# One column's transpose placed inside the first up unit, its copy shared by two engines, and the first up weights loaded in halves

## Chip, cores and metric

The kernel runs on one core of a Trainium2 chip. The metric is the device time of one execution in microseconds (us); of several executions the median is taken.

## What is computed

The input `x` has 2048 rows (the sequence) of 512 values. Each row is normalised, and the result is the sum of the input, a spectral filter and a gated MLP:

```
xn  = layernorm(x)                                   # over the 512 values
A   = irfft2(rfft2(xn) * (w_r + 1j * w_i))           # over rows and values
g   = xn @ w_gate        # 2048x512 @ 512x1792
u   = xn @ w_up          # 2048x512 @ 512x1792
B   = (gelu(g) * u) @ w_down                         # back to 2048x512
out = x + A + B
```

All inputs are bf16. The change touches the layer norm and the `g` and `u` products only in the order of their first pieces.

## The kernel before

The 2048 rows lie in 16 columns of 128 rows (`NC = 16`; column `c` holds rows `16p + c`). Every column is normalised with its rows on the partitions (`xn`) and then transposed into `xnT`, with the 512 values on the partitions in four blocks of 128 (`NE = 4`, index `e`), because the matmuls contract over the values. Columns 0 to 3 are transposed on TensorE (`f_T`, L346, into a PSUM tile `tp`) and copied to SBUF by VectorE or ScalarE (`f_Tc`, L351). The other twelve are transposed by DMA (L450).

The gated MLP is cut into units (`unit`, L465). A unit takes `n` columns and `m` blocks of 128 of the 1792 hidden values: it computes a gate part (`g_ps`) and an up part (`u_ps`) on TensorE, the gelu on ScalarE (`ge`, L498) and the product on VectorE (`hT`, L503). `g_ps` and `u_ps` have two PSUM buffers each: the gelu gives a `g_ps` buffer back and the product a `u_ps` buffer. The list `todo` (L530) gives the order: unit 0 is column 0 with hidden blocks 0 to 3, unit 1 is column 1 with the same blocks, units 2 and 3 are columns 0 and 1 with blocks 4 and 5 and then 6 and 7, and then come columns 2 and 3 and the rest. Unit 0 runs `mm_half` (L488), which goes over the value blocks `e` in two halves; every other unit runs `split`, which calls `mm` (L480), with the hidden block outside and `e` inside.

The spectral filter (forward transforms, groups of frequencies, inverse transform) is put between the units later on, and the down product closes the kernel (L811).

The order of each engine's instructions is written by a small planner (`Plan`, L135). Every step has an engine, a duration, a latency, a key and its dependencies; `t_min` is the earliest time and holds an expected landing time of the data (`LAND`, `WG_LAND`, `WU_LAND`, L309). The planner simulates and picks the ready step with the lowest key; the chip then runs each engine's list strictly in that order. The planner gives no times to the chip, only the order.

The opening (L274) is outside the planner. SyncE (SP) issues nearly all loads in the order written. ScalarE issues the first gate weights. Waits that are added when the program is built make a DMA wait, before it is issued, for an earlier one: eight completion semaphores go round, so that in the kernel before the load of columns 2 and 3 waits for column 0, the gate weights 512 to 1023 for column 1, and the up weights 512 to 1023 for the first quarter of the first up weights. TensorE runs 37 matmuls on zeros (L307) while it waits for data.

The steps near the change, as the list of each engine has them before:

- TensorE: transposes of column 0, six matmuls on zeros (L322), gate 0, up 0 (16 matmuls each), four transposes of column 1, gate 1, up 1, gate 2, up 2, eight transposes of columns 2 and 3, gate 3 and so on without another transpose.
- VectorE: statistics and normalisation of columns 0 and 1 (L337 to L343), one copy of the transposed column 1, statistics of columns 2 and 3, the products of units 0 and 1, normalisation of columns 2 and 3, the product of unit 2.
- ScalarE: two square roots (L392) and the copies of column 0 (L352), then a load of the gelu table and the gelus of units 0, 1 and 2.
- GpSimd: the inverse root for columns 2 and 3 (L355, L359), between their statistics and their normalisation.

```
for e in range(NE):
    load_w(Wu_sb, 0, 512, e=e)
...
t = add("PE", 0.23, lambda: f_T(1, 0, NE), [o["xn1"]], key=-1998, lat=0.45, acq=("S",))
...
v("copyt", lambda: f_Tc(1, 0, NE), 0.5, ["t"])
```

Of the kernel before, what the change touches and what calls it, by code (L numbers as in the profile page):

```python
# [17 lines left out]
S = 2048  # L18
# [3 lines left out]
NE = 4  # L22
# [112 lines left out]
class Plan:  # L135
# [6 lines left out]
    def add(self, eng, occ, fn, deps=(), key=0.0, lat=None, slack=0.0, t_min=0.0, acq=(), rel=(), after=None):  # L142
        lat = occ + 0.25 if lat is None else lat
        op = Op(len(self.ops), eng, occ, lat, fn, [d for d in deps if d is not None], key, slack, t_min, acq, rel,
                after)
        self.ops.append(op)
        return op
# [54 lines left out]
def kernel(  # L202
# [11 lines left out]
    nc = tc.nc  # L214
# [17 lines left out]
    Wg_sb = pc.tile([P, NE, DF], BF16, name="Wg_sb")  # L232
    Wu_sb = pc.tile([P, NE, DF], BF16, name="Wu_sb")
# [14 lines left out]
    def load_consts(first, last):  # L248
        a, b = ccols[first][0], sum(ccols[last])
        nc.sync.dma_start(out=CT[:, a:b], in_=cap[:, a:b])  # L250


    def load_x(c0, n, eng=nc.sync):
        eng.dma_start(out=x_t[:, c0:c0 + n, :], in_=x_v[:, c0:c0 + n, :])

    def load_w(a, b, eng=nc.sync):
        nc.sync.dma_start(out=Wg_sb[:, :, a:b], in_=wg_v[:, :, a:b])
        eng.dma_start(out=Wu_sb[:, :, a:b], in_=wu_v[:, :, a:b])
# [15 lines left out]
    def opening():  # L274
        nc.vector.memset(spin[:], 0.0)
        nc.vector.memset(eps_t[:], EPS)
        nc.vector.memset(minus_half[:], -0.5)
        U = nc.gpsimd
        U.memset(ident_t[:], 1.0)
        U.affine_select(out=ident_t[:], in_=ident_t[:], pattern=[[-1, P]], compare_op=ALU.is_equal, fill=0.0,  # L280
                        base=0, channel_multiplier=1)
        nc.scalar.activation(out=warm[:], in_=eps_t[:], func=AF.Sqrt, bias=eps_t[:], scale=1.0)
        load_x(0, 1)
        load_x(1, 1)
        load_w(Wg_sb, 0, 512, nc.scalar, e=slice(0, 2))
        load_w(Wg_sb, 0, 512, nc.scalar, e=slice(2, 4))
        for e in range(NE):
            load_w(Wu_sb, 0, 512, e=e)
        load_x(2, 2)
        load_w(Wg_sb, 512, 1024)  # L290
        load_w(Wu_sb, 512, 1024)
        load_x(4, 4)
        load_w(Wg_sb, 1024, DF)
        load_w(Wu_sb, 1024, DF)
        load_x(8, 4)
        nc.sync.dma_start(out=RF_t[:], in_=rf_d.rearrange("p (c k) -> p c k", c=NC))
        load_x(12, 4)
        nc.sync.dma_start(out=idx_t[:], in_=nc.inline_tensor(idx_np, name="spec_rows").ap())
        load_consts("F0", "L0")
        load_consts("I0", "M0")  # L300
        for T, w_in in ((TR, A_w_r), (TI, A_w_i)):
            rows = w_in.rearrange("(kb a h g) k -> h kb a (g k)", kb=NC, h=2, a=8)
            Tf = T.rearrange("p j k -> p (j k)")
            for h in range(2):
                nc.sync.dma_start(out=Tf[64 * h:64 * h + 64, W:8 * W], in_=rows[h, :, 0:4, W:8 * W])
        for k in range(37):
            nc.tensor.matmul(sp_ps[:, :P], lhsT=spin[:], rhs=spin[:], start=True, stop=True)  # L307

    LAND = {0: 2.9, 1: 4.5, 2: 7.2, 3: 7.2}  # L309
    LAND.update({c: 11.5 if c < 8 else 17.5 if c < 12 else 20.5 for c in range(4, NC)})  # L310
    WG_LAND = [5.0] * 4 + [8.6] * 4 + [13.2] * 6
    WU_LAND = [6.7] * 4 + [10.0] * 4 + [15.2] * 6
    RF_LAND = 19.0

    ident = ident_t[:]
# [10 lines left out]
    add = plan.add  # L326
    V, A, T_ = nc.vector, nc.scalar, nc.tensor
# [18 lines left out]
    def f_T(c, e0, n):  # L346
        tiles["T", c, e0] = tp = ps.tile([P, n, P], BF16, name="tp", tag="S", bufs=4)
        for e in range(n):
            T_.transpose(tp[:, e], xn[:, c, (e0 + e) * P:(e0 + e + 1) * P], ident)  # L349

    def f_Tc(c, e0, n, copy=V.tensor_copy):  # L351
        copy(out=xnT[0][:, e0:e0 + n, c, :], in_=tiles["T", c, e0][:])  # L352
# [14 lines left out]
        U.tensor_tensor(out=b, in0=mv[:, c0:c0 + n, 0], in1=rstd[:, c0:c0 + n], op=ALU.mult)  # L367
        U.tensor_scalar(out=b, in0=b, scalar1=-1.0, scalar2=None, op0=ALU.mult)  # L368

    xn_op, xT_op = {}, {}  # L370

    def first_two():
        o = {}

        def v(k, fn, occ, deps=(), lat=None, t_min=0.0):
            o[k] = add("DVE", occ, fn, [o[d] for d in deps], key=-2000 + len(o), lat=lat, t_min=t_min,
                       after=o.get("last"))
            o["last"] = o[k]

        def T(c, h):  # L380
            o["T", c, h] = add("PE", 0.12, lambda: f_T(c, 2 * h, 2), [o["xn", c, h]], key=-2000 + 2 * c + h,
                               lat=0.36, acq=("S",))

        def xn_(c, h):
            v(("xn", c, h), lambda: f_norm_v(c, 256 * h, 256), 0.27, [("recip", c)], lat=0.4)

        def stats(c):
            v(("stats", c), lambda: f_stats(c), 0.6, t_min=LAND[c], lat=0.7)

        def mean(c):  # L390
            v(("mean", c), lambda: f_mean(c), 0.17, [("stats", c)])
            o["root", c] = add("ACT", 0.31, lambda: A.activation(  # L392
                out=rstd[:, c:c + 1], in_=mv[:, c, 1:2], func=AF.Sqrt, bias=eps_t[:], scale=1.0),
                [o["mean", c]], key=-2000 + c)

        def recip(c):
            v(("recip", c), lambda: V.reciprocal(out=rstd[:, c:c + 1], in_=rstd[:, c:c + 1]), 0.15, [("root", c)])

        stats(0)
        mean(0)  # L400
        recip(0)
        xn_(0, 0)
        xn_(0, 1)
        stats(1)
        mean(1)
        T(0, 0)
        T(0, 1)
        add("PE", 0.33, spin_on, [o["T", 0, 1]], key=-1500, lat=0.33, after=o["T", 0, 1])
        table = add("ACT", 1.3, lambda: None, [o["root", 1]], key=-1500, lat=1.3)
        xT_op[0, 0], xT_op[0] = (  # L410
            add("ACT", 0.36, lambda h=h: f_Tc(0, 2 * h, 2, A.copy), [o["T", 0, h]], key=-1990 + h, lat=0.48,
                rel=("S",)) for h in range(2))
        recip(1)
        xn_op[0] = o["xn", 0, 1]
        v("xn1", lambda: f_norm_v(1, 0, D), 0.33, [("recip", 1)], lat=0.45)
        t = add("PE", 0.23, lambda: f_T(1, 0, NE), [o["xn1"]], key=-1998, lat=0.45, acq=("S",))
        o["t"] = t
        v("copyt", lambda: f_Tc(1, 0, NE), 0.5, ["t"])
        o["copyt"].rel = ("S",)
        xT_op[1] = o["copyt"]  # L420
        xn_op[1] = o["xn1"]
        return o["copyt"]

    ROOT = 1.1
    chain_end = first_two()
# [39 lines left out]
    def unit(k, c0, n, f0, m=1):  # L465
        sb, o, w = c0 // 4, (c0 % 4) * P, n * P
# [18 lines left out]
                    T_.matmul(b[name][:, f], lhsT=W_[:, e, (f0 + f) * P:(f0 + f + 1) * P], rhs=rhs[:, e, :],  # L485
                              start=(e == 0), stop=(e == NE - 1))

        def mm_half(s, name="g_ps", tag="G", W_=Wg_sb):  # L488
            if s == 0:
                b[name] = ps.tile([P, m, w], F32, name=name, tag=tag, bufs=2)  # L490
            for e in (2 * s, 2 * s + 1):
                for f in range(m):
                    T_.matmul(b[name][:, f], lhsT=W_[:, e, (f0 + f) * P:(f0 + f + 1) * P], rhs=rhs[:, e, :],  # L493
                              start=(e + f == 0), stop=(e == NE - 1), skip_group_check=True)
# [10 lines left out]
        occ = m * {1: 0.228, 2: 0.437, 4: 0.863}[n]  # L505
        src = [xT_op[c] for c in range(c0, c0 + n)]
        def split(name, tag, W_, key, t, h):
            o = None
            for f in range(0, m, h):
                o = add("PE", occ * h / m, lambda f=f: mm(name, tag, W_, range(f, f + h)), [o] if f else src, key=key,  # L510
                        lat=occ * h / m + 0.3, acq=() if f else (tag,), t_min=t[f0 + f + h - 1])
            return o

        if k == 0:
            g = add("PE", occ / 2, lambda: mm_half(0), [xT_op[0, 0]], key=1000, acq=("G",), t_min=WG_LAND[0])
            g = add("PE", occ / 2, lambda: mm_half(1), [xT_op[0], g], key=1000.1, lat=occ / 2 + 0.3)
            u = add("PE", occ / 2, lambda: mm_half(0, "u_ps", "U", Wu_sb), [g], key=1000.5, acq=("U",), t_min=6.2)
            u = add("PE", occ / 2, lambda: mm_half(1, "u_ps", "U", Wu_sb), [u], key=1000.6, lat=occ / 2 + 0.3,
                    t_min=WU_LAND[0])
        else:  # L520
            g = split("g_ps", "G", Wg_sb, 1000 + k, WG_LAND, m)
            u = split("u_ps", "U", Wu_sb, 1000.5 + k, WU_LAND, (2, m, 1)[k] if k < 3 else m)
        ge = add("ACT", {1: 0.28, 2: 0.36, 4: 0.5}[n * m], f_ge, [g], key=-1000 + k,
                 lat={1: 0.38, 2: 0.48, 4: 0.7}[n * m], acq=("ge",), rel=("G",))
        h = add("DVE", {1: 0.21, 2: 0.34, 4: 0.61}[n * m], f_h, [ge, u], key=-1000 + k, rel=("U", "ge"))
# [354 lines left out]
```

## Time and profile before

| | |
|---|---|
| median of 7 runs | 178.89 us (178.75 to 179.29) |
| the profiled execution | 178.77 us |
| its span in the profile | 177.1 us |
| TensorE busy | 172.7 us (98% of the span) |
| VectorE busy | 115.6 us (65%) |
| ScalarE busy | 96.5 us (54%) |
| GpSimd busy | 17.0 us (10%) |
| moved by DMA | 19.35 MB |

The profile is of one execution. Its span, from the first to the last instruction recorded, is 177.1 us, and 178.77 − 177.1 = 1.7 us of its time lie around the span. TensorE (PE) is busy from about 1 us to the end, so the busy shares tell little here: what counts is where TensorE stands still. "PEld" is the load of a matmul's weights, which runs beside the matmul ahead of it. "SPq" is the issuing of DMAs by SP. L numbers are lines of the kernel before.

### The profile page before, as it was taken

To read this page: it belongs to the slowest core of one execution; us is meant where nothing else is said; L and a number is where in the kernel's file an instruction comes from. 1 tells how busy PE (TensorE), PEld (TensorE's weight loads), DVE (VectorE), ACT (ScalarE), POOL (GpSimd) and SP (SyncE) were. 2 spreads that over 40 slices of the span, in tenths; PEclk is the share of its full clock that TensorE was granted. 3 is DMA by queue.
4 is the path that set the end of the run, shared out by engine and by line. 5 is a ranking of instruction groups with operands and counts; after the bars stand their busy time and mean duration, and the time that the engine had idled before them with its cause. 6 is when DMAs were issued, how large, how long until landed. Compare 5 with 4: busy or idle time off the path is not lost.

```text
span 177.1 us, 3131 instructions
## 1 busy us (share of the span) xinstructions
PE 172.7 (98%) x1145; PEld 96.7 (55%) x1145; DVE 115.6 (65%) x253; ACT 96.5 (54%) x172; POOL 17.0 (10%) x38
## 2 busy tenths in 40 slices
PE   7899999999999999999999999999999999999993
PEld 7788845464545554555555544454445445444463
DVE  2688799988434599998799999543516325345333
ACT  4633389798746999799999955452112111211200
POOL 1020260406760000000000000000000000000000
DMA  5999965453817802111201520200122222221212
GB/s 149 325 365 403 356 158 91 101 107 45 247 39 234 299 4 59 44 45 35 59 14 47 152 61 0 59 0 4 58 90 89 76 76 61 88 88 60 81 41 59
DMA packets 21359, 19.35 MB, mean 109 GB/s; under 512 B 8480, under 2 KB 20000, under 8 KB 21344
## 3 DMA queue, kind: packets, MB, share of 16 engines
q1 hardware_dynamic: 20384, 17.31, 33.1%
q0 software_dynamic: 416, 1.32, 2.6%
q10 hardware_dynamic: 544, 0.52, 1.1%
q8 instruction: 9, 0.15, 0.3%
q14 instruction: 6, 0.05, 0.1%
HBM read 13.38 MB, written 2.10 MB: 87 GB/s over the span
## 4 chain that ended last, share of the span: by engine, by line
PE 98%; DVE 1%; issue 0%
PE y_ps L815 27%; PE g_ps L485 27%; PE u_ps L485 27%; PE sp_ps L307 2%; PE yp L766 2%; PE gp L736 2%; PE bp L575 2%; PE dp L633 2%; PE y_ps L819 2%; PE ep L642 2%; PE tp L349 1%; PE g_ps L493 1%; PE u_ps L493 1%; DVE xnT L352 0%; PE sp_ps L322 0%; DVE y_sb L822 0%
## 5 line engine op out<-in xcount | busy, mean ns | idle before, releaser
L485 PE MATMUL g_ps<-xnT,Wg_sb 128*128 128x512 bf16 (+2 forms) x256 | 56.5, 349 | 0.5 <-DVE xnT L352 0.5
L485 PE MATMUL u_ps<-xnT,Wu_sb 128*128 128x512 bf16 (+2 forms) x256 | 56.6, 349 | 0.1
L815 PE MATMUL y_ps<-Wd_sb,hT 128*128 128x512 bf16 (+2 forms) x252 | 51.1, 355 | 0.0
L503 DVE TENSOR_TENSOR hT<-u_ps,ge 128x512 bf16<-128x512 f32 x56 | 38.5, 688 | 18.5 <-PE u_ps L485 14.9
L498 ACT ACTIVATE ge<-g_ps 128x512 bf16<-128x512 f32 x56 | 33.8, 604 | 21.3 <-PE g_ps L485 18.7
L815 PEld LDWEIGHTS <-hT 128*128 128x128 bf16 x252 | 23.2, 98 | 22.4
L485 PEld LDWEIGHTS <-Wu_sb 128*128 128x128 bf16 x256 | 23.9, 98 | 21.1 <-DMA Wu_sb<-in_B_w_up_dram 0.3
L485 PEld LDWEIGHTS <-Wg_sb 128*128 128x128 bf16 x256 | 23.8, 98 | 20.5 <-issue 0.6
L772 ACT CAST yf<-yp 128x512 bf16<-128x512 f32 x16 | 9.3, 586 | 40.5 <-PE yp L766 40.5
L822 DVE TENSOR_TENSOR y_sb<-y_ps,y_sb 128x512 bf16<-128x512 f32 (+2 forms) x18 | 11.1, 631 | 30.0 <-PE y_ps L819 30.0
L647 ACT CAST E<-ep 64x512 bf16<-64x512 f32 x32 | 18.6, 580 | 1.3 <-PE ep L642 0.8
L337 DVE BATCH_NORM_STATS2 stats<-x_t 128x6 f32<-128x512 bf16 x16 | 10.5, 677 | 3.5 <-DMA x_t<-in_A_x_dram 3.5
L447 ACT ACTIVATE xn<-x_t,nb,rstd 128x512 bf16<-128x512 bf16 x12 | 9.5, 814 | 2.3 <-POOL nb L368 2.2
L545 ACT CAST Gs<-gp 128x512 bf16<-128x512 f32 x16 | 8.9, 592 | 1.0 <-PE gp L736 0.9
L545 ACT CAST ds<-dp 128x512 bf16<-128x512 f32 x16 | 9.0, 597 | 0.6 <-PE dp L633 0.5
L545 ACT CAST Bs<-bp 128x512 bf16<-128x512 f32 x16 | 8.6, 610 | 0.5 <-PE bp L575 0.5
L778 DVE TENSOR_TENSOR lv<-yf 128x512 bf16<-128x512 bf16 x16 | 6.1, 422 | 1.5 <-ACT yf L772 0.6
L766 PEld LDWEIGHTS <-Gs 128*128 128x128 bf16 x64 | 4.8, 98 | 3.5
L785 DVE TENSOR_TENSOR yt<-lv 128x512 bf16<-128x512 bf16 x16 | 6.1, 422 | 0.3
L819 PE MATMUL y_ps<-yt,RI_t 128*128 128x512 bf16 (+2 forms) x18 | 6.1, 355 | 0.0
L766 PE MATMUL yp<-CT,Gs 128*128 128x128 bf16 x64 | 6.0, 219 | 0.0
L736 PEld LDWEIGHTS <-F 128*128 128x128 bf16 x64 | 4.5, 98 | 2.6
(67 smaller groups left out, 122.9 us busy)
## 6 DMA issues: line engine op xcount, KB each, us to landing
F<-F SPq DMA_DIRECT2D x32, 64.0 KB, 2.0
y_sb<-in_A_x_dram SPq DMA_DIRECT2D x16, 128.0 KB, 2.1
out_dram<-y_sb SPq DMA_DIRECT2D x15, 128.0 KB, 1.7
Wd_sb<-in_B_w_down_dram SPq DMA_DIRECT2D x1, 1792.0 KB, 7.6
x_t<-in_A_x_dram SPq DMA_DIRECT2D x3, 512.0 KB, 11.1
Wg_sb<-in_B_w_gate_dram SPq DMA_DIRECT2D x1, 768.0 KB, 9.1
Wu_sb<-in_B_w_up_dram SPq DMA_DIRECT2D x1, 768.0 KB, 10.7
Wg_sb<-in_B_w_gate_dram ACTq DMA_DIRECT2D x2, 256.0 KB, 3.8
```

Source lines behind the costliest of these rows:

```text
L337: V.bn_stats(out=st[:], in_=x_t[:, c, :])
L447: xn_op[c] = add("ACT", 0.72, lambda c=c: A.activation(out=xn[:, c, :], in_=x_t[:, c, :], func=AF.Identity, bias=nb[:, c:c + 1], scale=rst ...
L485: T_.matmul(b[name][:, f], lhsT=W_[:, e, (f0 + f) * P:(f0 + f + 1) * P], rhs=rhs[:, e, :], start=(e == 0), stop=(e == NE - 1))
L498: A.activation(out=b["ge"][:], in_=b["g_ps"][:], func=AF.Gelu_apprx_tanh)
L503: V.tensor_tensor(out=hT_of(sb, f0, m, o, w), in0=b["u_ps"][:], in1=b["ge"][:], op=ALU.mult)
L545: A.copy(out=o, in_=i)
L647: A.copy(out=b["E"][64 * h:64 * h + 64, r], in_=b["ep", h][64 * r:64 * r + 64])
L766: T_.matmul(t[:, q], lhsT=late["G"][:, q, c0 + j], rhs=IQ[q], start=(q == 0), stop=(q == 3), skip_group_check=True)
L772: A.copy(out=b["yf"][:, j], in_=b[j][:])
L815: T_.matmul(b[o][:], lhsT=hT_of(sb, f, 1, cl * P, P)[:, 0], rhs=Wd_sb[:, f, o:o + w], start=(f == 0), stop=False)
L819: T_.matmul(b[o][:], lhsT=late["RI"][:, c, :], rhs=late["yt"][:, c, o:o + w], start=False, stop=True)
L822: V.tensor_tensor(out=b["y"][:, o:o + w], in0=b[o][:], in1=b["y"][:, o:o + w], op=ALU.add)
```

## The change

Three edits.

1. The opening loads the first up weights in two pieces of 256 KB (blocks `e` 0 and 1, then 2 and 3) in place of four of 128 KB. The loads of columns 8 to 11 and of columns 12 to 15 are each cut into two. Since the semaphores go round eight loads, this also shifts which load waits for which: the gate weights 512 to 1023 now wait for no load, the up weights 512 to 1023 for column 0, and columns 4 to 7 for column 1.
2. The four transposes of column 1 become two pairs, placed inside up 0: four matmuls of up 0 (`e = 0`), the four transposes, the other twelve matmuls of up 0. The first pair is copied by VectorE (128x256), the second by ScalarE (128x256). In ScalarE's list that copy stands ahead of the load of the gelu table.
3. Gate 1 runs `mm_part` with `e` outside, in two halves: the first needs only the first pair's copy, the second needs both.

The planner's landing times are edited as well, and so the order of later steps (statistics of columns 4 to 15, spectral steps among the units) comes out differently: on VectorE from the statistics of column 4 on, on TensorE from the thirteenth unit on. TensorE's list has the same number of instructions in both kernels, 2292.

```diff
-        load_w(Wg_sb, 0, 512, nc.scalar, e=slice(0, 2))
-        load_w(Wg_sb, 0, 512, nc.scalar, e=slice(2, 4))
-        for e in range(NE):
-            load_w(Wu_sb, 0, 512, e=e)
+        for T, q in ((Wg_sb, nc.scalar), (Wu_sb, nc.sync)):
+            for e in (0, 2):
+                load_w(T, 0, 512, q, e=slice(e, e + 2))
...
-        load_x(8, 4)
+        load_x(8, 2)
+        load_x(10, 2)
...
-        load_x(12, 4)
+        load_x(12, 2)
+        load_x(14, 2)
...
-    LAND = {0: 2.9, 1: 4.5, 2: 7.2, 3: 7.2}
+    LAND = {0: 2.65, 1: 4.6, 2: 7.7, 3: 7.7}
...
-    WG_LAND = [5.0] * 4 + [8.6] * 4 + [13.2] * 6
-    WU_LAND = [6.7] * 4 + [10.0] * 4 + [15.2] * 6
+    WG_LAND = [5.0] * 4 + [9.1] * 4 + [13.2] * 6
+    WU_LAND = [7.2] * 4 + [10.4] * 4 + [15.2] * 6
...
-        t = add("PE", 0.23, lambda: f_T(1, 0, NE), [o["xn1"]], key=-1998, lat=0.45, acq=("S",))
-        o["t"] = t
-        v("copyt", lambda: f_Tc(1, 0, NE), 0.5, ["t"])
-        o["copyt"].rel = ("S",)
-        xT_op[1] = o["copyt"]
+        o["t", 0] = add("PE", 0.12, lambda: f_T(1, 0, 2), [o["xn1"]], key=1000.54, lat=0.3, acq=("S",))
+        o["t", 1] = add("PE", 0.12, lambda: f_T(1, 2, 2), [o["xn1"]], key=1000.55, lat=0.3, acq=("S",),
+                        after=o["t", 0])
+        between.update(o)
+        v("copyt0", lambda: f_Tc(1, 0, 2), 0.25, [("t", 0)], lat=0.4)
+        o["copyt1"] = add("ACT", 0.4, lambda: f_Tc(1, 2, 2, A.copy), [o["t", 1], table], key=-1400)
+        o["copyt0"].rel = o["copyt1"].rel = ("S",)
+        xT_op[1, 0] = o["copyt0"]
+        xT_op[1] = o["copyt1"]
         xn_op[1] = o["xn1"]
-        return o["copyt"]
+        return o["copyt0"]
...
-        def mm_half(s, name="g_ps", tag="G", W_=Wg_sb):
-            if s == 0:
+        def mm_part(e0, e1, name="g_ps", tag="G", W_=Wg_sb):
+            if e0 == 0:
                 b[name] = ps.tile([P, m, w], F32, name=name, tag=tag, bufs=2)
-            for e in (2 * s, 2 * s + 1):
+            for e in range(e0, e1):
...
-            g = add("PE", occ / 2, lambda: mm_half(1), [xT_op[0], g], key=1000.1, lat=occ / 2 + 0.3)
-            u = add("PE", occ / 2, lambda: mm_half(0, "u_ps", "U", Wu_sb), [g], key=1000.5, acq=("U",), t_min=6.2)
-            u = add("PE", occ / 2, lambda: mm_half(1, "u_ps", "U", Wu_sb), [u], key=1000.6, lat=occ / 2 + 0.3,
-                    t_min=WU_LAND[0])
+            g = add("PE", occ / 2, lambda: mm_part(2, NE), [xT_op[0], g], key=1000.1, lat=occ / 2 + 0.3, t_min=6.3)
+            u = add("PE", occ / 4, lambda: mm_part(0, 1, *up), [g], key=1000.5, acq=("U",), t_min=6.5)
+            between["t", 0].deps.append(u)
+            u = add("PE", occ / 4, lambda: mm_part(1, 2, *up), [u, between["t", 1]], key=1000.6)
+            u = add("PE", occ / 2, lambda: mm_part(2, NE, *up), [u], key=1000.7, lat=occ / 2 + 0.3, t_min=WU_LAND[0])
+        elif k == 1:
+            g = add("PE", occ / 2, lambda: mm_part(0, 2), [xT_op[1, 0]], key=1001, acq=("G",))
+            g = add("PE", occ / 2, lambda: mm_part(2, NE), [*src, g], key=1001.3, lat=occ / 2 + 0.3)
+            u = split(*up, 1001.5, WU_LAND, m)
```

More of the change, by code (lines that the diff above doesn't have):

```diff
@@ L368, in bias @@
         U.tensor_scalar(out=b, in0=b, scalar1=-1.0, scalar2=None, op0=ALU.mult)
-    xn_op, xT_op = {}, {}
+    xn_op, xT_op, between = {}, {}, {}
     def first_two():
@@ L512, in split @@
             return o
+        up = "u_ps", "U", Wu_sb
         if k == 0:
-            g = add("PE", occ / 2, lambda: mm_half(0), [xT_op[0, 0]], key=1000, acq=("G",), t_min=WG_LAND[0])
-            g = add("PE", occ / 2, lambda: mm_half(1), [xT_op[0], g], key=1000.1, lat=occ / 2 + 0.3)
-            u = add("PE", occ / 2, lambda: mm_half(0, "u_ps", "U", Wu_sb), [g], key=1000.5, acq=("U",), t_min=6.2)
-            u = add("PE", occ / 2, lambda: mm_half(1, "u_ps", "U", Wu_sb), [u], key=1000.6, lat=occ / 2 + 0.3,
-                    t_min=WU_LAND[0])
+            g = add("PE", occ / 2, lambda: mm_part(0, 2), [xT_op[0, 0]], key=1000, acq=("G",), t_min=WG_LAND[0])
+            g = add("PE", occ / 2, lambda: mm_part(2, NE), [xT_op[0], g], key=1000.1, lat=occ / 2 + 0.3, t_min=6.3)
[7 more added lines that the diff above has]
+            u = split(*up, 1001.5, WU_LAND, m)
         else:
             g = split("g_ps", "G", Wg_sb, 1000 + k, WG_LAND, m)
-            u = split("u_ps", "U", Wu_sb, 1000.5 + k, WU_LAND, (2, m, 1)[k] if k < 3 else m)
+            u = split("u_ps", "U", Wu_sb, 1000.5 + k, WU_LAND, 1 if k == 2 else m)
         ge = add("ACT", {1: 0.28, 2: 0.36, 4: 0.5}[n * m], f_ge, [g], key=-1000 + k,
```

## The prediction

> **What bounds the kernel now.** I read the page's chain of work that ended last, then TensorE's waits, then the timeline of the first 14 us. Gains and losses under 0.2% (0.36 us) count here as no change: about what a measurement of this kernel can tell.
>
> ```profile
> PE 98%; DVE 1%; issue 0%
> ```
> The chain is TensorE from end to end, so only a TensorE stop can be won. From 5 us on its waits, and those of its weight loads, are few:
> ```profile
> PE g_ps L485 <- DVE xnT L352: 0.5, 1, 0.5
> PEld L485 <- DMA Wu_sb<-in_B_w_up_dram: 0.3, 1, 0.3
> ```
> The timeline shows both (start, length; mixed engines):
> ```profile
> 6.72 0.41 DVE L343 TENSOR_SCALAR xn<-x_t,mv,rstd 128x512 bf16<-128x512 bf16 x1
> 6.89 1.06 PE L493 MATMUL u_ps<-xnT,Wu_sb 128*128 128x128 bf16 x16
> 7.78 0.39 PE L349 MATMUL tp<-ident_t,xn 128*128 128x128 bf16 x4
> 8.20 0.42 DVE L352 COPY xnT<-tp 128x512 bf16<-128x512 bf16 x1 [1.07 <-PE tp L349]
> 8.68 1.05 PE L485 MATMUL g_ps<-xnT,Wg_sb 128*128 128x128 bf16 x16 [0.52 <-DVE xnT L352]
> 10.46 1.04 PE L485 MATMUL g_ps<-xnT,Wg_sb 128*128 128x256 bf16 x8
> 11.55 1.05 PE L485 MATMUL u_ps<-xnT,Wu_sb 128*128 128x256 bf16 x8
> 12.44 0.61 PE L349 MATMUL tp<-ident_t,xn 128*128 128x128 bf16 x8
> 12.89 1.04 PE L485 MATMUL g_ps<-xnT,Wg_sb 128*128 128x256 bf16 x8
> ```
> The transposes of column 1 stand behind all of up 0, though their input is ready at 6.72+0.41 = 7.13. TensorE then has nothing until the copy is out: starts are 0.0556 us apart (16 in 0.89), so gate 1 could start at 8.00 and starts at 8.68: 0.68 lost. Second stop: gate 2 starts at 10.46, its 8 matmuls take 0.87 (12.89 to 13.76 for gate 3), so up 2 could start at 11.34 and starts at 11.55: 0.21 lost, to the up weights 512 to 1023. After that TensorE never waits. Gain 1 therefore runs into stop 2 at once unless those weights also come earlier.
>
> [...] the loads that SP issued at 3.60, 4.72 and 5.93 landed 4.0, 5.4 and 5.6 us later, at 7.6, 10.1 and 11.5, in order. [...] Here an SP issue takes 0.4 to 0.5 us. [...]
>
> **The change, part by part.**
>
> *Transposes inside up 0.* The four up matmuls of `e` = 0 start at 6.89; the next slot is 7.11. The transposes need xn at 7.13 plus 0.06 (column 0: input done 5.33, weights loaded from 5.39), so they start at 7.20: 0.09 of stop. Four in 0.24, then twelve up matmuls from 7.44 to 8.11. Cost of moving: zero instructions, the same four.
>
> *Copies.* A pair ends about 0.29 after its first transpose starts, so 7.49 and 7.60; the copier starts 0.04 later. VectorE: 128x256 is not shown; bounds 0.21 (half of 0.42) and 0.42[...]. ScalarE: 0.37, column 0's copy: 7.64 to 8.01. Both are out before gate 1's slot at 8.11, so gate 1 starts at 8.11 instead of 8.68: 0.57 won. Cover gone means a start at the copy's end plus 0.05; even 0.42 (7.95) is hidden. `e` outside in gate 1 changes no count.
>
> *The wait this adds: ScalarE's table.* ScalarE's list now has the copy ahead of the table load, which before ran at 6.50 in idle time. Queued behind the copy: table 8.03 to 9.31, gelu 0 until 9.92 (8.39 before), gelu 1 until about 10.44. Who waits: gate 2 needs gelu 0's PSUM buffer, 9.92+0.05 = 9.97 against its slot 8.11+2x0.89 = 9.89: 0.08 of stop. VectorE needs gelu 0 for the first product:
> ```profile
> 9.95 0.66 DVE L503 TENSOR_TENSOR hT<-u_ps,ge 128x512 bf16<-128x512 f32 x1
> 10.74 0.69 DVE L503 TENSOR_TENSOR hT<-u_ps,ge 128x512 bf16<-128x512 f32 x1
> 11.35 0.73 DVE L343 TENSOR_SCALAR xn<-x_t,mv,rstd 128x512 bf16<-128x512 bf16 x2
> ```
> Before, the second product waited for up 1 (its matmuls end at 10.63). Now up 1 ends at 10.06, so both run on: 9.96 to 10.62, 10.62 to 11.31, normalisations 11.23 to 11.96. The first transpose of column 3 thus starts at 12.02 and gate 3, four transposes on, at 12.27: 0.61 earlier than 12.89. This is a ceiling, not a loss.
>
> *Loads.* Two issues fewer, and the semaphores turn: the waits of 0.7 and 0.8 us ahead of the gate and up weights 512 to 1023 go. At the issue pace of 0.47 they leave SP at about 3.1 (4.72 before) and 3.6 (5.93); column 0 landed by 3.26, so the new wait costs nothing. The bytes ahead are the same. But the DMA engines were not full just then:
> ```profile
> 7.00:8.00 1.00, 1.00 (x21) 1.00 (x19) 0.13 (x1) 0.99 (x2) 0.00 (x0) 1.00 0.85 241
> 8.00:9.00 1.00, 0.48 (x9) 0.36 (x7) 0.80 (x2) 0.39 (x1) 0.00 (x0) 1.00 1.01 300
> 9.00:10.00 1.00, 1.00 (x22) 1.00 (x19) 1.00 (x5) 0.23 (x1) 0.00 (x0) 1.00 1.06 376
> ```
> The last columns are DMA share and GB/s. Two slices at 376 would move 752 KB, they moved 541: 211 KB, 0.56 us. So the up weights land at 11.53−0.56 = 10.97. Bounds: unchanged, 11.53, if the early queue only spreads the engines apart; 7.60 + 1.05 MB at 376 = 10.4 if nothing later slips in between. Up 2's slot is 9.97+0.87 = 10.84; at 10.97+0.02 it starts at 10.99, 0.56 earlier than 11.55.
> The first up weights' second half is needed at 7.61; the last quarter landed at 6.93 (issued 3.13, 3.8 us), with the same bytes ahead. Columns 2 and 3 may land up to 0.5 late (8.1): hidden, since their statistics, 1.5 us, are due at 9.9. Gate weights 512 to 1023, 10.1 before, are needed at 9.9 and gain as the up weights do: 9.6.
>
> *Later on SP.* The constants now wait for the 768 KB weight loads (16.0 and 18.1) instead of 11.5 and 12.75; their first reader in the chain is at 54.7. The spectral tables' loads go out perhaps 2 us later, needed at 40. The transposing DMAs wait for these semaphores: the fourth went out at 28.69 and landed 2.4 us later, 31.1, and columns 4 to 7 are first used at 33.0: 1.9 us of cover, 1.3 once TensorE is earlier. If gone, each later us is a us. Halved x loads: VectorE waited 1.2 us for columns 8 to 11 at 19.39, and the product behind that ended at 20.67 for an up part at 20.75; a half lands no later, so this cover grows. GpSimd's list is unchanged. I take the re-planned rest at zero, bounds −0.1 and +0.5.
>
> **Sum.** Up 2 starts 0.56 earlier, nothing later eats it, and TensorE is full to the end: 178.77 − 0.56 = 178.21 for the profiled execution. It lies 0.12 under the median, so 178.89 − 0.56 = 178.33; with 0.05 for small new joins, 178.4.
>
> **Rivals.**
> - *The second stop stays.* Up weights land at 11.2 to 11.53: up 2 wins 0 to 0.35, middle 0.15, 178.75. For: all 16 engines are near full from 4 to 7 us, and transfers queued early share them. Against: the 241 and 300 GB/s. The change not doing what it says for the total is this case's end: 0.57 won at gate 1 and given back at up 2. Chance 0.24.
> - *ScalarE's table becomes the bound: slower.* Place: between the copy and gelu 0. Gate 3 is later than before once gelu 0 ends more than 0.61 after my 9.92, at 10.53. [...] For: the whole front of VectorE's list hangs on gelu 0. [...] With milder delays here: chance 0.13.
> - *Forecast*, up weights in time: 0.63.
>
> **How the numbers follow.** The forecast is faster; of the second, 0.05 faster and 0.19 same; of the third, 0.11 slower and 0.02 same. Faster 0.68, same 0.21, slower 0.11. Low end: the ceiling 0.61, plus 0.1 of the rest and 0.1 of scatter among the runs, 178.1. High end: the second stop whole, 178.9. Outside stay the third case and some of each end, 0.2 together.
>
> **What would show it.** Right: gate 1 at 8.1 with no wait on the copy; a table load at 8.0; gelu 0 ending at 9.9; the first two products back to back; up 2 at 10.8 to 11.1; gate 3 at 12.2 to 12.4; no TensorE wait after. Wrong: a stop inside up 0 (second half of the weights late), up 2 still waiting at 11.5, a transpose of column 3 waiting for its normalisation past 12.3, or a new stop behind 20 us.

## The result, and the profile after

| | before | after |
|---|---|---|
| median, run side by side | 179.05 us (178.54 to 180.09, 62 runs) | 179.68 us (179.34 to 181.85, 25 runs) |
| the profiled execution | 178.77 us | 179.92 us |
| its span | 177.1 us | 178.2 us |
| start of gate 3 | 12.89 us | 14.04 us |

The ratio is 1.0041 with a 95% interval of 1.0029 to 1.0054: the change makes the kernel slower, by about 0.7 us. I had forecast 178.4. The two profiled executions lie further apart, 1.15 us: that of before was 0.28 under its median, that of after 0.24 over. What follows reads these two; a second profile of the changed kernel, further down, has gate 3 at 13.64 instead of 14.04.

The chain of work that ended last, on the page of the kernel after, no longer is TensorE from end to end:
```profile
PE 91%; DMA 5%; SPq 1%; issue 0%; DVE 0%
```
Listed in order of time (start, length, what), its longest piece is one load, that of the up weights 512 to 1023: issued at 3.68, it holds the chain for 9 us.
```profile
3.68 8.98 DMA Wu_sb<-in_B_w_up_dram
```
TensorE's waits (us in total, times, longest) of the kernel after are now both for weights:
```profile
PE g_ps L490 <- DMA Wg_sb<-in_B_w_gate_dram: 1.2, 1, 1.2
PE u_ps L490 <- DMA Wu_sb<-in_B_w_up_dram: 0.4, 1, 0.4
```
The timeline of the kernel after (start, length):
```profile
7.21 0.40 PE L350 MATMUL tp<-ident_t,xn 128*128 128x128 bf16 x4
7.54 0.29 DVE L353 COPY xnT<-tp 128x256 bf16<-128x256 bf16 x1 [0.38 <-PE tp L350]
7.65 0.37 ACT L353 COPY xnT<-tp 128x256 bf16<-128x256 bf16 x1 [1.14 <-PE tp L350]
8.04 1.28 ACT L503 ACT_TABLE_LOAD   x1
8.12 1.06 PE L498 MATMUL g_ps<-xnT,Wg_sb 128*128 128x128 bf16 x16
9.01 1.06 PE L490 MATMUL u_ps<-xnT,Wu_sb 128*128 128x128 bf16 x16
9.33 1.08 ACT L503 ACTIVATE ge<-g_ps 128x512 bf16<-128x512 f32 x2
11.26 1.05 PE L490 MATMUL g_ps<-xnT,Wg_sb 128*128 128x256 bf16 x8 [1.19 <-DMA Wg_sb<-in_B_w_gate_dram]
12.71 1.05 PE L490 MATMUL u_ps<-xnT,Wu_sb 128*128 128x256 bf16 x8 [0.40 <-DMA Wu_sb<-in_B_w_up_dram]
13.59 0.61 PE L350 MATMUL tp<-ident_t,xn 128*128 128x128 bf16 x8
14.04 1.04 PE L490 MATMUL g_ps<-xnT,Wg_sb 128*128 128x256 bf16 x8
```
Down to gate 1 at 8.12 this is the forecast. Then gate 2, whose slot is 9.01+0.89 = 9.90, starts at 11.26 (1.36 lost), and up 2, whose slot is 11.26+0.87 = 12.13, at 12.71 (0.58 lost). Before, the two stops were 0.68 and 0.21. 1.36+0.58−0.68−0.21 = 1.05, with 0.1 up to and at the transposes inside up 0, is the 1.15 by which gate 3 is later. Nothing further on adds to it: the last matmul starts at 175.22 instead of 174.07, also 1.15.

The DMA view of the kernel after gives the loads (KB, us from issue to landing) that took 4.0, 5.4 and 5.6 us before:
```profile
x_t<-in_A_x_dram SPq DMA_DIRECT2D x1, 256.0 KB, 6.8
Wg_sb<-in_B_w_gate_dram SPq DMA_DIRECT2D x1, 512.0 KB, 8.0
Wu_sb<-in_B_w_up_dram SPq DMA_DIRECT2D x1, 512.0 KB, 9.0
```
They were issued at 2.69, 3.20 and 3.68, that is 0.9, 1.5 and 2.25 us earlier than before, and landed at 9.47, 11.21 and 12.66 instead of 7.60, 10.10 and 11.51: all three later. The stretches of 1 us (last columns DMA share and GB/s) say that the hole at 7 to 9 us, which I had meant to fill, is still there, 541 KB in these two us before and 543 KB now:
```profile
7.00:8.00 1.00, 1.00 (x20) 0.91 (x18) 0.45 (x2) 0.35 (x1) 0.00 (x0) 1.00 0.86 218
8.00:9.00 1.00, 1.00 (x22) 1.00 (x19) 0.00 (x0) 0.98 (x2) 0.00 (x0) 1.00 0.92 325
```
At a share of 0.86 the engines are occupied and yet move 218 GB/s: some packets take long. The packet records name them. The 128 packets of columns 2,3 (2 KB each) took 86 ns on average before, at most 105; after, 139 on average, 20 of them over 200 and one 859. Packets of 1 or 2 KB that take over 200 ns are called held from here on. The landing records have one entry for each of the 16 DMA engines. The first engine is done with columns 2,3 at 7.03 before and 7.06 after, the last at 7.60 and at 9.47. The lag stays: of the gate weights the first of the 16 shares is in at 8.62 and 8.71, the last at 10.10 and 11.21. Whether the same engines are last each time the records don't say. Here the matmuls waited for the last engine of their load: gate 2 starts at 11.26 and up 2 at 12.71, each 0.05 after it.

### The profile page after: what moved, and what is told of

It is laid out like the page before. It is cut to its first block, busy times and chain, and to the rows that moved or that the text cites. A ratio compares the mean times of both kernels' runs of the same rounds, so it can differ in the third digit from the quotient of the medians.

```text
span 178.2 us, 3133 instructions
## 1 busy us (share of the span) xinstructions
PE 172.8 (97%) x1145; PEld 96.8 (54%) x1145; DVE 115.7 (65%) x253; ACT 96.8 (54%) x173; POOL 17.2 (10%) x38
## 4 chain that ended last, share of the span: by engine, by line
PE 91%; DMA 5%; SPq 1%; issue 0%; DVE 0%
PE y_ps L826 27%; PE u_ps L490 26%; PE g_ps L490 26%; DMA Wu_sb<-in_B_w_up_dram 5%; PE bp L586 2%; PE dp L644 2%; PE yp L777 2%; PE gp L747 2%; PE y_ps L830 2%; PE ep L653 2%; SPq L270 1%; SPq L266 1%; PE tp L350 0%; DVE y_sb L833 0%
## 5 line engine op out<-in xcount | busy, mean ns | idle before, releaser
L490 PE MATMUL g_ps<-xnT,Wg_sb 128*128 128x512 bf16 (+1 forms) x240 | 55.3, 358 | 1.2 <-DMA Wg_sb<-in_B_w_gate_dram 1.2
L490 PEld LDWEIGHTS <-Wg_sb 128*128 128x128 bf16 x240 | 22.9, 98 | 21.9 <-DMA Wg_sb<-in_B_w_gate_dram 1.4
L338 DVE BATCH_NORM_STATS2 stats<-x_t 128x6 f32<-128x512 bf16 x16 | 10.4, 676 | 3.9 <-DMA x_t<-in_A_x_dram 3.9
L568 DVE TENSOR_TENSOR A<-xn 128x1024 bf16<-128x1024 bf16 x8 | 5.3, 678 | 1.0 <-ACT xn L452 1.0
```

The costliest lines, as they stand in the source:

```text
L338: V.bn_stats(out=st[:], in_=x_t[:, c, :])
```

## The experiments

Most kernels in one table; e16, e17 and e18 follow in the text. It gives the times of issue by SP (gate weights, up weights 512 to 1023, and the load after them), the mean time of the 128 column packets, and the last engine's landing, all of one profiled execution each; the ratio is of many. "Again" is a second profile of the same kernel.

| kernel | issued: gate, up, next | column packets, ns | landed: columns 2,3, gate, up | ratio to before |
|---|---|---|---|---|
| before | 4.72, 5.93, 6.35 | 86 | 7.60, 10.10, 11.51 | 1 |
| e1_order | 4.69, 5.86, 6.29 | 90 | 8.17, 9.95, 11.37 | 0.9987 |
| e11_quarters_gate3_first | 4.81, 5.95, 6.37 | 95 | 7.89, 10.22, 11.65 | 0.9979 |
| e3_halves_paced | 4.91, 6.34, 7.08 | 91 | 7.72, 9.55, 11.27 | 1.0001 |
| e9_pads_behind_columns | 4.59, 6.22, 6.91 | 88 | 7.58, 9.04, 11.43 | 0.9999 |
| e10_gate3_first | 4.63, 6.39, 7.03 | 86 | 7.68, 9.40, 11.02 | 0.9974 |
| e14_only_gate_early | 3.20, 6.42, 6.99 | 108 | 7.88, 9.30, 12.28 | 1.0003 |
| e13_three_pads | 6.26, 6.93, 7.35 | 93 | 7.83, 10.74, 12.12 | 1.0041 |
| e8_one_pad | 3.52, 4.64, 6.14 | 147 | 9.22, 10.78, 12.26 | 1.0035 |
| after | 3.20, 3.68, 4.77 | 139 | 9.47, 11.21, 12.66 | 1.0041 |
| e15_changed_again | 3.20, 3.68, 4.92 | 160 | 9.19, 10.77, 12.26 | |
| e2_loads | 3.20, 3.68, 4.93 | 153 | 9.38, 10.94, 12.43 | 1.0023 |
| e12_hold_short | 3.20, 3.68, 7.24 | 144 | 9.24, 10.72, 12.15 | 1.0035 |
| e7_hold_weights | 3.20, 4.22, 5.25 | 169 | 9.52, 11.03, 12.41 | 1.0048 |
| again (e7b) | 3.20, 3.68, 4.64 | 162 | 9.79, 11.37, 12.74 | |
| e5_hold | 3.20, 3.68, 10.16 | 109 | 8.35, 9.90, 11.25 | 1.0071 |
| again (e5b) | 3.20, 3.68, 11.11 | 161 | 9.47, 10.85, 12.19 | |

**Which half of the change.** e1_order keeps the engines' order of the changed kernel and puts the loads of the kernel before back:
```diff
-        for T, q in ((Wg_sb, nc.scalar), (Wu_sb, nc.sync)):
-            for e in (0, 2):
-                load_w(T, 0, 512, q, e=slice(e, e + 2))
+        load_w(Wg_sb, 0, 512, nc.scalar, e=slice(0, 2))
+        load_w(Wg_sb, 0, 512, nc.scalar, e=slice(2, 4))
+        for e in range(NE):
+            load_w(Wu_sb, 0, 512, e=e)
...
-        load_x(8, 2)
-        load_x(10, 2)
+        load_x(8, 4)
...
-        load_x(12, 2)
-        load_x(14, 2)
+        load_x(12, 4)
```


> The loads of the kernel before, with everything else of the changed kernel: transposes inside up 0, both copies, gate 1 in halves. Theory L (the loads made it slower): the loads land as before, columns 2 and 3 at 7.6, gate weights 512 to 1023 at 10.1, up weights 512 to 1023 at 11.5 us. Gate 1 starts at 8.1, gate 2 at about 10.1, up 2 again at 11.55, so the time is that of the kernel before, ratio 0.999 to 1.001. Rival E (the order on the engines, with gelu 0 behind the copy and the table load, makes it slower): up 2 or gate 3 later than before, ratio about 1.004, as the changed kernel.

e2_loads is the mirror image: the kernel before, with the four load edits of the changed kernel and nothing else.

> The kernel before with the loads of the changed kernel alone: first up weights in halves, columns 8 to 15 in four loads. Theory L: columns 2 and 3 land near 9.4, gate weights 512 to 1023 near 11.2, up weights 512 to 1023 near 12.7; gate 2 waits until 11.2 and up 2 until 12.7, ratio 1.004 to 1.007. Rival E: the landings stay within 0.2 us of 7.6, 10.1 and 11.5, ratio 0.999 to 1.001.

Measured: 0.9987 (0.9978 to 0.9996) and 1.0023 (1.0011 to 1.0036). With the old loads the order of the engines is a small gain; the loads are the loss. The two do not simply add: the whole change measured 1.0041 (1.0029 to 1.0054), and whether the new order costs something once the weights are late is open, as this interval overlaps that of e2_loads. The timeline of e1_order shows why the gain is small, as up 2 still waits for its weights, and gate 3 is only 0.15 earlier than 12.89:
```profile
11.41 1.05 PE L489 MATMUL u_ps<-xnT,Wu_sb 128*128 128x256 bf16 x8 [0.19 <-DMA Wu_sb<-in_B_w_up_dram]
12.30 0.61 PE L349 MATMUL tp<-ident_t,xn 128*128 128x128 bf16 x8
12.74 1.04 PE L489 MATMUL g_ps<-xnT,Wg_sb 128*128 128x256 bf16 x8
```

**Halves, or the waits that they turn.** e3_halves_paced is the changed kernel with two loads of 128 bytes put in, which only move the round of eight semaphores on, so that the later loads wait as before:
```diff
+        for k in range(2):
+            nc.sync.dma_start(out=pad_t[0:1, 64 * k:64 * k + 64], in_=x_v[0:1, 0, 64 * k:64 * k + 64])
         load_x(2, 2)
         load_w(Wg_sb, 512, 1024)
```


> The changed kernel with two loads of 128 bytes behind the halves of the first up weights, so that the eight semaphores turn as in the kernel before and the same waits stand ahead of the loads of columns 2 and 3 and of the gate and up weights 512 to 1023; halves stay halves. Theory P (the earlier issue makes the landings late): up weights 512 to 1023 issued at about 5.9 and landed at 11.5, ratio 0.999 to 1.001. Rival H (pieces of two blocks are themselves slow to load, or throw the engines apart): landing near 12.7, ratio about 1.004.

Measured: 1.0001 (0.9981 to 1.0022), landings within 0.12 us of before, or earlier. The halves are harmless; the lost waits are the harm. One thing is mixed into the ratios of the kernels with extra loads: their end is 0.3 to 0.4 us longer (see the last experiment), about 0.002 of the ratio. So e3_halves_paced has gate 3 at 12.64, 0.25 earlier than before, and loses this again at the end. e8_one_pad and e13_three_pads change the 2 in `range` to 1 and 3.

> The changed kernel with one 128-byte load between the first up weights and columns 2,3 instead of two, so the waits before the later issues move on by one: half the pacing. If the delay grows with how far the queue runs ahead, up weights 512 to 1023 land between 11.4 and 12.6 us and the ratio is 1.001 to 1.003. If one particular wait is what matters, it is all or nothing: 11.3 us and 1.000, or 12.6 us and 1.004.

> Three 128-byte loads ahead of columns 2,3 (zero, one and two gave up weights 512 to 1023 at 12.66, 12.26 and 11.27 us): the columns wait for column 0, the gate weights for the first half of the gate weights, the up weights for the next half, and so on. If less queue is better without end, up weights land under 11.2 us, ratio under 1.000. If two was enough, the same within 0.2 us and 0.999 to 1.001. If pacing now starves the engines, gate weights land over 10.2 us or columns 2,3 over 8.3, ratio 1.001 to 1.004.

Measured: 1.0035 (1.0020 to 1.0051) and 1.0041 (1.0027 to 1.0055). With one, the landings are those of the changed kernel's second profile, so in that execution it brings nothing; but some 0.4 us of its time is the longer end, and the ratio leaves room for a partial relief. Whether there is a threshold or a slope stays open. Three starve the engines: the gate weights leave SP only at 6.26, and the stretch from 7 to 8 us of e13_three_pads is half empty (share 0.51, 80 GB/s):
```profile
7.00:8.00 1.00, 1.00 (x22) 1.00 (x20) 0.43 (x2) 0.40 (x2) 0.00 (x0) 1.00 0.51 80
```

**Which early issue.** e9_pads_behind_columns puts the two small loads behind `load_x(2, 2)`; e14_only_gate_early puts them one load further down, between the gate and the up weights 512 to 1023.

> The two 128-byte loads stand behind columns 2,3 instead of ahead of them: columns 2,3 go as early as in the changed kernel (issued near 2.7 us), the weights 512 to 1023 and all behind as late as in the kernel with the pads ahead. If the lost pacing of the weights and of what is behind them is the cause, columns 2,3 land by 8.2 us, gate weights by 9.9, up weights by 11.4, ratio 0.998 to 1.001. If the early columns load is itself the harm, it lands near 9 us and the up weights over 12, ratio over 1.002.

> The two 128-byte loads stand between the gate and the up weights 512 to 1023: columns 2,3 and these gate weights are issued as early as in the changed kernel (2.69 and 3.20 us), the up weights and all behind them as late as in the kernel before (near 6.2 us). If it is the second load of weights queued before the columns are moved that harms, columns 2,3 land by 8.2 us, gate weights by 10.0, up weights by 11.5: ratio 0.998 to 1.001. If early gate weights alone are the harm, columns 2,3 land at 8.4 to 9.8, gate weights over 10.5, up weights over 12: ratio 1.003 to 1.005.

Measured: 0.9999 (0.9984 to 1.0015) and 1.0003 (0.9986 to 1.0020). Columns 2,3 may go at 2.69 and the gate weights at 3.20 without harm: the gate weights of e14 land at 9.30, 1.9 us before those of the changed kernel issued at the same moment. The DMA view of e14 has these gate weights and then its up weights (KB, us from issue to landing):
```profile
Wg_sb<-in_B_w_gate_dram SPq DMA_DIRECT2D x1, 512.0 KB, 6.1
Wu_sb<-in_B_w_up_dram SPq DMA_DIRECT2D x1, 512.0 KB, 5.9
```
What differs between e14 and the changed kernel is the up weights, 6.42 against 3.68, and all behind them. In e14 15 of the 16 engines have brought the up weights by 10.62 and one by 12.28, which costs that execution a stop at up 2; its 14 runs scatter from 178.51 to 180.21.

**The up weights themselves, or what stands behind them.** These keep all three early issues and hold back the rest by a one-element copy on GpSimd, which the next load must wait for. In e5_hold it reads the gate weights 512 to 1023 and holds columns 4 to 7 and all behind; in e7_hold_weights columns 4 to 7 go free and the weights 1024 to 1791 are held; in e12_hold_short it reads the second half of the first up weights. The cut shows all three; each kernel has only the added line that bears its name.
```diff
         load_w(Wu_sb, 512, 1024)
+        U.tensor_copy(out=x_t[0:1, 4, 0:1], in_=Wg_sb[0:1, 0, 512:513])      # e5_hold
+        U.tensor_copy(out=x_t[0:1, 4, 0:1], in_=Wu_sb[0:1, 2, 0:1])          # e12_hold_short
         load_x(4, 4)
+        U.tensor_copy(out=Wg_sb[0:1, 0, 1024:1025], in_=Wg_sb[0:1, 0, 512:513])  # e7_hold_weights
         load_w(Wg_sb, 1024, DF)
```


> The changed kernel with the load of columns 4 to 7, and all that SP issues behind it, held back until the gate weights 512 to 1023 have landed (GpSimd copies one element of them into the target of that load first). Theory Q (what lies in the rings behind the up weights 512 to 1023 slows them): columns 2 and 3 land at about 7.6, the up weights 512 to 1023 at 10.4 to 11.0, gate 3 starts at 12.3 to 12.5, ratio 0.997 to 0.998. Rival P alone (the early issue of the two 512 KB loads themselves is enough): columns 2 and 3 land near 9.4 and the up weights near 12.5, ratio about 1.004.

> The changed kernel with only the gate and up weights 1024 to 1791 (and what SyncE's queue has behind them) held until the gate weights 512 to 1023 have landed; columns 4 to 7 are free to go. Theory A, the weights queued behind make up the delay: up weights 512 to 1023 land near 11.3 us as in the kernel that held everything, and, since the columns are not held, nothing is paid at 40 us: ratio 0.998 to 1.000. Theory B, columns 4 to 7 are the harm: up weights 512 to 1023 stay near 12.5 us, ratio 1.003 to 1.006. A third way, the hold is paid later as it was with the columns held: up weights near 11.3 us and yet a ratio over 1.003.

> The changed kernel with columns 4 to 7 and all behind them held only until the second half of the first up weights has landed (near 6.9 us, where the kernel before issues them at 6.35), while columns 2,3 and the weights 512 to 1023 are issued as early as in the changed kernel. If the depth of the queue behind them is what harms, columns 2,3 land by 8.4 us, gate weights by 10.0, up weights near 11.3, and nothing is paid at 40 us: ratio 0.998 to 1.001. If issuing the weights 512 to 1023 early is already the harm as soon as anything follows before they land, gate weights land near 11 and up weights over 12: ratio over 1.003.

e5_hold made me believe in the depth of the queue for a while: up weights at 11.25. It was one execution. Its second profile has 12.19, and e12_hold_short, which holds the rest until 7.24, later than the kernel before issues it, has 12.15 and a ratio of 1.0035 (1.0020 to 1.0049). Its up weights took 8.5 us, as against 5.9 in e14:
```profile
Wu_sb<-in_B_w_up_dram SPq DMA_DIRECT2D x1, 512.0 KB, 8.5
```

> A second look at the changed kernel with columns 4 to 7 and all behind them held until the gate weights 512 to 1023 have landed. If the depth of the queue behind is what harms, up weights 512 to 1023 land near 11.3 us again. If the first look was one lucky execution, they land over 12 us and columns 2,3 over 9, as with the short hold, which is the same kernel up to 7.2 us.

> A second look at the kernel that holds only the weights 1024 to 1791. In the first profile column 0 landed at 4.21 us instead of 2.9, which moved the whole opening. If that was an accident of one execution, column 0 lands near 2.9 us here; then columns 4 to 7 are the harm if up weights 512 to 1023 still land over 12 us, and the weights behind are it if they land near 11.3.

> The changed kernel once more, nothing edited. If the lag of single engines is a property of the order of the loads, columns 2,3 land last near 9.5 us (8.9 to 9.9), gate weights near 11.2, up weights near 12.7, as in the first profile, while the first of the 16 engines is done near 7.1, 8.7 and 10.4. If it was chance, they land more than 0.5 us from these.

These executions took 180.25, 180.30 and 179.53 us. In the second profile of the kernel that holds the weights column 0 lands at 2.97, so the 4.21 of the first was an accident, and the up weights are late with nothing but columns 4 to 7 behind them. The changed kernel repeats its lag within 0.45 us. So it is the early issue of the up weights, not what follows. Holding columns 4 to 7 that long has a price of its own (1.0071, 1.0049 to 1.0092): in both profiles of e5_hold TensorE loses time at 40 us, 0.9 and 0.55 us, and in neither of e7_hold_weights. The late columns are the likely cause, not a shown one, as e18 below loses 0.5 us at these matmuls without a hold:
```profile
40.81 0.87 PE L587 MATMUL bp<-RF_t,xf 128*128 128x128 bf16 x8 [0.30 <-ACT Bs L557]
```

**Which load suffers.** e16_weights_first puts `load_x(2, 2)` behind the two weight loads, e17_columns_singly cuts it into `load_x(2, 1)` and `load_x(3, 1)`.

> The changed kernel with the gate and up weights 512 to 1023 queued ahead of columns 2,3 (all three still issued by 4.2 us). If it is the columns' load that suffers from weights queued behind it, the weights now move undisturbed: gate weights land near 9.2 us and up weights near 10.6, and the columns near 11.5, undisturbed or not. If whichever load stands at that place suffers, the gate weights' packets of 1 KB take much more than 50 ns on average at 6 to 8 us, gate weights land over 10 us and up weights over 11.6. Either way columns 2,3 come late for their transposes, and the time is over 180 us.

> Columns 2 and 3 as two loads of 128 packets of 1 KB instead of one of 128 packets of 2 KB. The extra load turns the waits by one, as one pad did: gate weights 512 to 1023 issued near 3.6 us, up weights near 4.7, which with one pad gave columns 2,3 at 9.22, gate weights at 10.78 and up weights at 12.26 us. If the packet size doesn't matter, the same within 0.4 us. If long packets of 2 KB are what is held up, columns 2,3 land by 8.3 us, gate weights by 10.0, up weights by 11.5.

One execution each. e16_weights_first (issued 2.69, 3.20, columns 3.76) shows no held packet from 7 to 12 us, and the DMA engines are full where the kernels before and after have their hole:
```profile
7.00:8.00 1.00, 1.00 (x19) 0.86 (x17) 0.58 (x3) 0.00 (x0) 0.00 (x0) 1.00 1.08 377
8.00:9.00 1.00, 1.00 (x22) 1.00 (x20) 0.24 (x1) 0.92 (x2) 0.00 (x0) 1.00 1.10 364
```
Gate weights landed at 8.98, up weights at 10.46. The columns, at 11.13, moved just as freely (92 ns a packet) with other loads behind them, but far too late: VectorE stood on their statistics with the first products behind, and TensorE waited 1.9 us at up 2 for a `u_ps` buffer (180.76 us). So in this execution neither the weights in the first place nor the columns in a later one are held up; the columns in the first place are, when both weight loads are queued early behind them. e17_columns_singly landed columns at 8.70, gate weights at 10.15, up weights at 11.65, about 0.6 better than e8_one_pad, which issues them at nearly the same moments, and not as good as the paced kernels: between the two expectations. It does not settle the part of the packet size: its up weights left SP 0.3 later than those of e8_one_pad (4.95, 4.64), and the first execution of e5_hold landed early by chance.

**A version that beats both.** With the pacing back, what is left is up 2 waiting until 11.3. e10_gate3_first is e3_halves_paced with the planner told to expect these weights at 11.6 and to put the transposes of columns 2 and 3 off until 12.0, so that gate 3, whose weights are there, runs ahead of up 2. e11_quarters_gate3_first does the same to e1_order.
```diff
-    WU_LAND = [7.2] * 4 + [10.4] * 4 + [15.2] * 6
+    WU_LAND = [7.2] * 4 + [11.6] * 4 + [15.2] * 6
...
-            t = add("PE", 0.23, lambda c=c: f_T(c, 0, NE), [xn_op[c]], key=-880 + c, lat=0.5, acq=("S",))
+            t = add("PE", 0.23, lambda c=c: f_T(c, 0, NE), [xn_op[c]], key=-880 + c, lat=0.5, acq=("S",),
+                    t_min=12.0)
```


> The kernel with the pads ahead, and the planner told that the up weights 512 to 1023 are there at 11.6 us instead of 10.4, so that TensorE takes gate 3 (same gate weights, already there) ahead of up 2, and the transposes of columns 2,3 behind up 2. If the landing of the up weights near 11.3 us is the whole of what is left (a stop of 0.54 us at up 2), the stop goes: last matmul some 0.5 us earlier than with the pads alone, ratio 0.996 to 0.998. If another stop takes its place (the copies of columns 2,3, gelu), ratio 0.999 to 1.001.

> The loads of the kernel before (quarters), the order of the engines of the changed kernel, and gate 3 ahead of up 2 as in the run with the pads (0.9974). If the pads and halves add nothing of their own, the stop of 0.36 us at up 2 goes: last matmul near 173.4, ratio 0.996 to 0.998. If the halves give a gain, this is slower than the run with the pads by 0.1 to 0.3 us.

Measured: 0.9974 (0.9962 to 0.9987), 178.70 us against 179.08, and 0.9979 (0.9965 to 0.9992), 178.58 against 178.99: both faster than before, and not told apart. e11_quarters_gate3_first is not told apart from e1_order (0.9987) either; its last matmul starts at 173.68, that of e1_order at 173.92. The timeline of e10_gate3_first runs through, gates 2 and 3 in one piece:
```profile
9.87 1.91 PE L494 MATMUL g_ps<-xnT,Wg_sb 128*128 128x256 bf16 x16
11.61 0.60 PE L494 MATMUL u_ps<-xnT,Wu_sb 128*128 128x256 bf16 x4
12.05 0.61 PE L353 MATMUL tp<-ident_t,xn 128*128 128x128 bf16 x8
12.49 1.47 PE L494 MATMUL u_ps<-xnT,Wu_sb 128*128 128x256 bf16 x12
```
Its last matmul starts at 173.24, 0.83 before the 174.07 of the kernel before, but its span is only 0.4 shorter. Every kernel here with one to three loads more ends 3.3 to 3.4 us after that start, the others 3.0. e18_gate3_first_old_count makes the late x loads whole again, so that the count is the old one.

> The kernel with two 128-byte loads and gate 3 ahead of up 2, with columns 8 to 11 and 12 to 15 again in one load each, so that the number of loads is that of the kernel before and the last stores use the same two of the eight semaphores as there. Opening as in the kernel it is made from: up weights 512 to 1023 near 11.0 us, no stop at up 2, last matmul near 173.3. If the count of loads is what lengthens the end, the span is 3.0 us from the start of the last matmul, not 3.4, and the ratio 0.994 to 0.997. If the end is as long as before the change of count (3.4), the ratio is that of the parent, 0.997 to 0.998. If whole loads of four columns cost something at 14 to 20 us, a new wait shows there and the ratio is over 0.998.

Measured: 0.9979 (0.9964 to 0.9994). Its end is 3.0 us long, as expected of the count; but its last matmul starts at 173.90, mostly because 0.5 us went to the 16 matmuls `bp` at 39.14, which took 1.56 where e10_gate3_first has 1.06. In this execution what was won at the end was lost in the middle, and the version isn't better.

## Why the prediction was wrong, point by point

- *Transposes inside up 0*: right. Start 7.21 (forecast 7.20), gate 1 at 8.12 (8.11).
- *Copies*: right. VectorE 0.29 from 7.54, inside its bounds of 0.21 and 0.42; ScalarE 0.37 from 7.65.
- *ScalarE's table*: right. Table at 8.04 for 1.28, the first gelu at 9.33, right at its end, as before the change (6.50 for 1.28, gelu at 7.80). The second rival needed gelu 0 to end after 10.53; it ended at 9.93, and the rival fell. Its chance of 0.13 was my estimate: no trace showed a delay there.
- *Loads*: **this step failed**, in sign. I took the hole at 7 to 9 us for free capacity, because the queue seemed thin there, and counted 211 KB, 0.56 us, as won by issuing earlier. The up weights were to land at 10.97, with bounds of 10.4 and 11.53 (the landing before, 11.51 in the records); they landed at 12.66. The gate weights, 9.6 in the sum, landed at 11.21, columns 2,3, up to 8.1, at 9.47. About half of the hole was engine time taken by held packets (15 in these two us, 4.8 us beyond the 46 ns that is the median of the 1 KB packets from 6 to 12 us, or 0.30 us on each of 16 engines), as the very rows that I quoted could have told: the shares are 0.85 and 1.01 against 1.06 in the full stretch from 9 to 10 us, the rates 241 and 300 against 376 GB/s. The bytes were low, the occupation much less so: by the shares (1.06−0.85)+(1.06−1.01) = 0.26 us was free, not 0.56. That corrects the size but not the sign. The loss shows as engines drifting apart: the first shares of the gate and up weights landed 0.09 and 0.37 later than before, the last ones 1.11 and 1.15. I did name the danger, "if the early queue only spreads the engines apart", but took "unchanged, 11.53" as its worst case. The spread of columns 2,3 over the 16 engines went from 0.57 to 2.41 us, and the bound needed a side below nothing.
- *First up weights in halves*: right. The second half landed at 6.93, and up 0 never stopped for weights.
- *Gates and second stop*: the gain at gate 1 is real, 0.56 (forecast 0.57), but e1_order shows what it is worth with the old loads: 0.15 at gate 3, 0.9987, the mechanism and about the size of the first rival's case. The prediction's 178.4 needed weights that come earlier as well.
- *Later on SP*, at zero: right. All of the 1.15 is lost ahead of 14 us.

Neither rival came true: neither had the loads land later than before. The third way to slower was the wait that the change removes: the semaphore waits at 4.72 and 5.93 looked like idle time of a queue and were pacing.

Shown: the early issue of the up weights, with columns 2,3 at the head, is what delays (e14 against the changed kernel and e12); the halves, the order of the engines with the old loads, and the loads behind are not. Not shown: why a packet is held (up to 713 ns before the change and 859 after it), and why this spreads the engines so far. Held column packets, 20 and more of 128, go with two weight loads queued early behind the columns (8 in e14 and in the lucky execution of e5_hold), and there are none in e16_weights_first with the weights ahead of them. But holding as such is not new: before the change 15 packets of the weights were held between 7 and 12 us, and none of columns 2,3. What part the packet size plays is open too (e17).

## What to carry to other kernels

The hole in the bytes per us was worth 0.56 us here, but the share of the DMA engines left only 0.26 of it free; compare both columns before counting on one. The loads of the changed kernel were as late as the slowest of the 16 engines (gate 2 and up 2 start 0.05 after it), and a lag on one load was carried into the two that followed (2.41, 2.50 and 2.25 us between the first and the last engine). So issuing further ahead can make every load later (issued 0.9 to 2.25 us earlier, landed 1.1 to 1.9 later): bound such a step on both sides. Where a kernel can't get a load earlier, reorder the consumer: the three kernels that put gate 3, whose data is there, ahead of the wait are 0.2 to 0.3% faster than before. The new order inside up 0 is part of that gain.

## What I had not expected of the hardware

- Loads issued 0.9 to 2.25 us earlier landed 1.1 to 1.9 us later, with the same bytes ahead of them.
- Two loads of 128 bytes, 0.65 us of SP's time, took 1.4 us off the landing of the 512 KB behind them (12.66 to 11.27); a third put 0.85 back.
- One SP issue can be held up itself: the two issues of columns 8 to 11 took 3.34 us in the changed kernel and 1.33 in e3_halves_paced. What holds it is not shown.
- From the start of the last matmul to the end of the span it is 3.0 us with the old number of loads and 3.3 to 3.4 with one to three more.
